# When weight conversions may run ahead in the first four steps, and a third buffer for early queries and keys

## The chip, the cores and the metric

One core of a Trainium2 chip runs the whole program. Its engines are TensorE (PE, the matrix engine; PEld is its weight load), VectorE (DVE), ScalarE (ACT), GpSimd (POOL) and SyncE (SP, which here only issues DMAs). Each works through its own queue in order; they wait for each other by semaphores. The metric is the device time of one execution in microseconds (us). Before the change it is 867.95 us, the median of three runs.

## The reference

Windowed attention, then two feed-forward networks, all in float32:

```python
def _attn_ref(q, k, v):                      # (4, 8, 576, 64)
    scores = scale * np.matmul(q, k.transpose(0, 1, 3, 2))
    mask = (rel >= 0) & (rel < 64)           # rel = query position - key position
    scores = np.where(mask, scores, -1000000000.0)
    scores = scores - np.max(scores, axis=-1, keepdims=True)
    attn = np.exp(scores)
    attn = attn / (np.sum(attn, axis=-1, keepdims=True) + 1e-09)
    return np.matmul(attn, v).astype(np.float32)

def _moe_ref(x, w1, w2, w3, w_out):          # x: 2304 x 512, d_ff 1024
    h = (x @ w1) * (x @ w2) @ w3
    return (h @ w_out).astype(np.float32)

def _moe2_ref(x, w_in, w_out):               # d_ff 2048
    h = x @ w_in
    return ((h * (1.0 / (1.0 + np.exp(-h)))) @ w_out).astype(np.float32)
```

The weights reach the kernel as float64, and it turns them into float32 itself.

## The kernel before

**Stages.** `phase_w` multiplies w3 and w_out of the first network into one matrix w' (in the code `wp`), and computes the first 14 groups of attention beside it. `phase_a`, run for six blocks of 384 tokens, multiplies by w1, w2 and w', and the remaining groups of attention run inside it. The last loop is the second network. Nothing of the order is left to a scheduler: the whole program is under a manual schedule, and every engine's queue has the order in which the Python code emits the instructions.

**A chunk** (class `Chunk`) is one 128x512 piece of a float64 weight. Its steps are: a load of 512 KB from SP (`load`, tile `words`); two ACT instructions (L114, L115, tiles `cv_b` and `cv_r`); two DVE instructions (L125 into a PSUM tile `cv_z`, L128 back into `cv_b`); and an integer addition on POOL (L132). Pieces of w3 and w_out end there, as float32 (`w3x`/`q` and `wo`). Pieces of w1 and w2 (the list `order`, 16 of them) are split further into a rounded high part (ACT, L140) and a low part, the rest (L144, tile `hl`). `words`, `cv_b`, `cv_r` have a few buffers each.

**The line** is the list of chunks in the order of their conversion. `steps_to(n, lo, keep)` advances it: step t converts chunk t with ACT, chunk t-1 with DVE and POOL, and does the high part of chunk t-3 and the low part of chunk t-4. The engine of the low part is `lo[t % len(lo)]`; `phase_w` passes (vector, gpsimd), so that an even t has it on DVE and an odd t on POOL. `line.append(None)` puts in a place without a chunk. `ready[s]` is the number of steps after which the two chunks of step s of w' are converted; `loads_to` issues loads ahead of the steps.

**w'** is accumulated in 16 steps s of two halves each (`part` 0 and 1). Ahead of each half `phase_w` calls `steps_to`, then `halves_to`, which emits attention, then two matmuls of w' (L485). In the code before, the conversions are called up to one and a half to two steps ahead of the half at hand from the start.

**Attention** goes by groups g (128 queries, two heads). A group's even half emits: scores on PE (L265, tile `s`), mask and row maximum on DVE (L279, with its read-out into `nm`), values of group g-2 on PE (L339 to L341, tile `o`, one PSUM buffer), three transposes of group g-1 on PE (L312, tile `t`), its copy on ACT (L318, `pw`), and exponentials on ACT (L290). The odd half emits the sum, reciprocal and scaling on DVE (L298, L300, L302, which writes `sm`), the copy of finished values on ACT (L342, `xr`), which frees `o`, and the loads of queries and keys of group g+2 (L223 `qp`, L227 `kp`). The first 17 groups are computed in plain float32 (`plain(g)`); their queries share a tile tag with later groups and have two buffers, their keys have two buffers `k_p`.

SP has at most eight DMAs on the way here: each issue in its queue waits for a semaphore that an issue eight places earlier raises when it lands.

Of the kernel before, what the change touches and what calls it, by code (L numbers as in the profile page):

```python
# [9 lines left out]
F32 = mybir.dt.float32  # L10
# [20 lines left out]
W12_A, W12_B = 3, 13  # L31
# [11 lines left out]
def tile_window_attention_ffn(ctx, tc, qkv, vp, mask, ident, w1, w2, w3t, w_out, w_in, w_out2, out):  # L43
# [7 lines left out]
    nc = tc.nc  # L51
# [4 lines left out]
    att = late.enter_context(tc.tile_pool(name="att", bufs=2, side="right"))  # L56
# [92 lines left out]
    line = []  # L149
    done = {"load": 0, "step": 0}  # L150

    def loads_to(n):
        while done["load"] < min(n, len(line)):
            if line[done["load"]]:
                line[done["load"]].load()
            done["load"] += 1
# [35 lines left out]

    sm = [att.tile([128, 2, 192], F32, name=f"sm{i}", tag=f"sm{i}", bufs=1) for i in range(2)]
    k_lo = [att.tile([128, 384], F32R, name=f"klo{i}", tag=f"klo{i}", bufs=1) for i in range(2)]
    k_p = [att.tile([128, 384], F32, name=f"kp{i}", tag=f"kp{i}", bufs=1) for i in range(2)]
    v_p = [att.tile([128, 320], F32, name=f"vp{i}", tag=f"vp{i}", bufs=1) for i in range(3)]
    sums_of = [att.tile([128, 2, 2], F32, name=f"es{i}", tag=f"es{i}", bufs=1) for i in range(2)]
    for t in sums_of:
# [6 lines left out]
    def plain(g):  # L205


        return g < PLAIN
# [5 lines left out]
    def load_qk(g):  # L214
        if g < NG and g not in loaded:
            loaded.add(g)
            u, c = place(g)
            if not plain(g):
                qk_raw[g] = att.tile([128, 768], F32, name=f"qk{g}", tag="qk", bufs=2)
                nc.sync.dma_start(out=qk_raw[g], in_=qkv[u, c, :, 0:768])  # L220
                return
            qk_raw[g] = att.tile([128, 768], F32, name=f"qp{g}", tag="qkhi", bufs=2)[:, 0:128]
            nc.sync.dma_start(out=qk_raw[g], in_=qkv[u, c, :, 0:128])  # L223

            for h, hs in HEADS:
                n = slice(384 + h * 192, 576 + h * 192)
                nc.sync.dma_start(out=k_p[g % 2][hs, h * 192 : h * 192 + 192], in_=qkv[u, c, hs, n])  # L227

    def load_v(g):
        if g < NG and ("v", g) not in loaded:  # L230
# [30 lines left out]
    def scores(g):  # L261
        s_ps = psa.tile([128, 2, 192], F32, name=f"s{g}", tag="s")
        t = qk_raw.pop(g) if plain(g) else qk_st.pop(g)
        if plain(g):
            nc.tensor.matmul(s_ps, lhsT=t[:, 0:128], rhs=k_p[g % 2], start=True, stop=True)  # L265
        else:
            for h in range(2):

                nc.tensor.matmul(  # L269
                    s_ps[:, h], lhsT=t[:, 128 + h * 128 : 256 + h * 128],  # L270
                    rhs=t[:, 384 + h * 192 : 576 + h * 192], start=(h == 0), stop=False,
                )
            nc.tensor.matmul(s_ps, lhsT=t[:, 0:128], rhs=k_lo[g % 2], start=False, stop=True)  # L273
        nm = att.tile([128, 2], F32, name=f"nm{g}", tag="nm", bufs=2)
        rs = att.tile([128, 2], F32, name=f"rs{g}", tag="rs", bufs=2)
        fill(2)
        for h in range(2):

            nc.vector.tensor_tensor_reduce(  # L279
                out=sm[g % 2][:, h, :], in0=s_ps[:, h, :], in1=mask_sb[:, mask_kind(place(g)[0]), 64 - 64 * h : 256 - 64 * h],  # L280
                op0=ALU.add, op1=ALU.min, scale=-(D ** -0.5), scalar=3.0e38, accum_out=nm[:, h : h + 1],
            )
        fill()
        s_st[g] = (nm, rs)
# [75 lines left out]
    def half(h):  # L360

        g, odd = divmod(h, 2)
        if not odd:
            if g < NG:
                scores(g)
            if 2 <= g <= NG + 1:
                sums.append(values(g - 2))
            if 1 <= g <= NG:  # L370
                split_t(g - 1, transposes(g - 1))
            if g < NG:
                exps(g)
            if g >= 2 and (g - 2) % (3 * NPAIR) == 3 * NPAIR - 1:
                sums.pop()()
        else:
            if g < NG:
                normalise(g)
            if sums:
                sums.pop()()  # L380
            prep_qk(g + 2)
            if g < NG:
                prep_v(g)

            for x in range(g + 2, g + 5):
                if plain(x) and x > g + 2:
                    break
                load_qk(x)
            for x in range(g + 1, g + 4):
                if g < (x - 1 if plain(x - 3) else x - 3):  # L390
                    break
                load_v(x)
# [17 lines left out]
    def phase_w():  # L410
# [22 lines left out]
        ready, i12 = [], 0  # L433
        order = (0, 1, 2, 3, 8, 9, 10, 11, 4, 5, 6, 7, 12, 13, 14, 15)
        for s in range(16):
            if s < 8:
                add(None, w_out[s * 128 : (s + 1) * 128, :], wo[:, s])
            add_w3(s)
            ready.append(len(line) + 1)
            while i12 < W12_BY[s]:  # L440
                add_w12(order[i12])
                i12 += 1
# [1 line left out]
            add_w12(order[i12])  # L444
            i12 += 1
        drain()
        ready += [W12_B + 24 + (4 if W12_B == 16 else 0)] * 2

        for t in k_p + [f32(t) for t in k_lo]:
            for h, hs in HEADS:  # L450
# [1 line left out]
        loads_to(2)  # L452
        load_qk(0)
        nc.sync.dma_start(out=mask_sb[:, 1], in_=mask[:, 1])
        loads_to(3)
        nc.sync.dma_start(out=id_sb, in_=ident)
        load_v(0)
        load_qk(1)
        loads_to(5)
        nc.sync.dma_start(out=mask_sb[:, 0], in_=mask[:, 0])  # L460
        load_v(1)
        loads_to(6)
        load_v(2)
        steps_to(ready[0])
        nc.sync.dma_start(out=mask_sb[:, 2], in_=mask[:, 2])
        half(0)
        halves[0] = 1
        acc, split_done = {}, set()
        for s in range(16):
            sw, j = divmod(s, 8)  # L470
            loads_to(ready[s + 2] + (3 if s > 1 else 0))
            if j == 0:
                for i in range(4):
                    acc[i] = accumulator(f"accw{sw}_{i}", [128, 512])
            for part in range(2):
                first = ready[s + 1 if s else 0]
                steps_to(first + (ready[s + 2] - first) * (part + 1) // 2, (nc.vector, nc.gpsimd), 3)
                halves_to(min(W_HALVES, 2 + W_HALVES * (2 * s + part + 1) // 32))
                for c in range(4):
                    if halves[0] >= min(W_HALVES, 6 * c + 10) and (0, c) not in split_done:  # L480
                        split_done.add((0, c))
                        split_x(0, c)
                fill(3)
                for i in (0, 1) if part == 0 else (2, 3):
                    nc.tensor.matmul(  # L485
                        acc[i], lhsT=w3x[s % 7][:, i * 128 : (i + 1) * 128], rhs=wo[:, j],
                        start=(j == 0), stop=(j == 7),
                    )
                    if j == 7:
                        n = sw * 4 + i  # L490
                        wp[n] = slot(f"wp{n}", f"w{16 + n}", [2, 512], F32R)
                        split(wp[n][:, 0], wp[n][:, 1], acc[i], "act", "dve")
# [58 lines left out]
    with tc.manual_schedule():  # L551
        xr = slot("xr", "xr", [4, NB])
        phase_w()
        new_pt()
        phase_a(0, lambda n: steps_to(W12_B + 24 + (n + 1) * (20 - W12_B) // 6, (nc.vector, nc.gpsimd)))
        for blk in range(1, NBLK - 1):
            phase_a(blk, lambda n: None)
        late.close()
# [206 lines left out]
```

## Time and profile before

| what | value |
|---|---|
| time, median of 3 runs (lowest to highest) | 867.95 us (867.81 to 868.38) |
| time of the execution that was profiled | 867.71 us |
| its span in the profile | 865.9 us |
| PE busy in the span | 846.7 us (98%) |
| `phase_w` (to the first matmul of L513) | 0 to 97.19 us |
| PE busy in the first 33.1 us | 20.63 us |
| PE busy from 33.1 to 97.2 us | 61.57 us |
| PE busy from 97.2 to 865.9 us | 764.49 us |
| DVE, ACT, POOL busy in the span | 436.5, 497.0, 444.7 us |

The profile shows one execution. Its span lies 1.8 us under that execution's time; the rest is around it. A timeline row has the start in us from the span's beginning, the duration in us, engine, line, operation, `out<-in`, shapes, how many instructions are merged, and in brackets the idle time of the engine just before with what ended it. Busy time of matmuls is modelled.

### The profile page before, as it was taken

The numbers are of one execution on the slowest core, as the hardware profiler recorded it, in microseconds if no ns is written. First come the engines' busy times: TensorE is split into PE (matmuls) and PEld (weight loads), VectorE is DVE, ScalarE is ACT, GpSimd is POOL, SyncE is SP. The second block draws the span as 40 slices with busy tenths as digits, with TensorE's granted clock in tenths as the row PEclk, the third lists the DMA queues.
The fourth block names the chain that finished last, engine by engine and source line by source line (L and its number), as shares of the span: only waits on it lengthen the run. The fifth ranks groups of instructions, "written<-read, shape, count | busy, mean of one in ns | idle before, by whom it ended". The sixth has DMA issues, their size and how long they took to land.

```text
span 865.9 us, 13392 instructions
## 1 busy us (share of the span) xinstructions
PE 846.7 (98%) x4362; PEld 736.0 (85%) x4362; DVE 436.5 (50%) x1160; ACT 497.0 (57%) x1243; POOL 444.7 (51%) x494
## 2 busy tenths in 40 slices
PE   5899999999999999999999999999999999999998
PEld 2445799999999999999998888888888888888896
DVE  5978877677777777675465884111111111111111
ACT  5889878788788788786766774222222222222222
POOL 4768666566666666665685886223322232223222
PEclk9999999999999999999999999999999999999999
DMA  8989333323323333320787100200020002000100
GB/s 304 323 276 276 102 103 102 120 92 110 111 92 121 110 98 116 111 92 34 249 326 272 74 1 0 98 1 1 0 98 1 1 0 74 1 1 0 49 1 25
DMA packets 43205, 85.84 MB, mean 99 GB/s; under 512 B 4864, under 2 KB 22528, under 8 KB 43136
## 3 DMA queue, kind: packets, MB, share of 16 engines
q1 hardware_dynamic: 37088, 75.55, 26.3%
q10 hardware_dynamic: 6048, 9.44, 3.0%
q8 instruction: 35, 0.57, 0.3%
q14 instruction: 34, 0.28, 0.1%
HBM read 75.53 MB, written 9.44 MB: 98 GB/s over the span
## 4 chain that ended last, share of the span: by engine, by line
PE 86%; issue 1%; DVE 1%; ACT 1%; POOL 0%; POOLq 0%; ACTq 0%; DVEq 0%
PE h L636 23%; PE o L655 23%; PE ab L513 22%; PE x L533 12%; PE t L312 2%; PE o L346 1%; PE s L269 1%; PE s L273 1%; PE o L347 1%; ACT sm L290 0%; POOL g L82 0%; DVE sm L302 0%; DVE a L521 0%; ACT p L79 0%; DVE cv_b L128 0%
## 5 line engine op out<-in xcount | busy, mean ns | idle before, releaser
L82 POOL TENSOR_TENSOR g<-sg,g 128x512 fp32r<-128x512 f32 (+1 forms) x80 | 94.7, 1184 | 249.7 <-ACT g L79 235.1
L636 PE MATMUL h<-x2t,hl 128*128 128x512 f32 (+1 forms) x960 | 213.3, 371 | 0.0
L655 PE MATMUL o<-hl,g 128*128 128x512 f32 x864 | 211.2, 391 | 0.1
L636 PEld LDWEIGHTS h<-x2t,hl 128*128 128x128 f32 x960 | 169.4, 188 | 33.9
L642 DVE TENSOR_TENSOR sg<-h,sg 128x512 f32<-128x512 f32 (+1 forms) x80 | 51.1, 638 | 288.2 <-ACT sg L641 288.2
L655 PEld LDWEIGHTS o<-hl,g 128*128 128x128 f32 x864 | 160.9, 188 | 35.6 <-POOL g L82 0.5
L641 ACT ACTIVATE sg<-h 128x512 f32<-128x512 f32 (+1 forms) x80 | 44.4, 554 | 194.8 <-PE h L636 194.7
L513 PE MATMUL ab<-xa,hl 128*128 128x384 f32 x576 | 118.9, 341 | 0.0
L513 PE MATMUL ab<-xb,hl 128*128 128x384 f32 x576 | 115.4, 334 | 0.0
L513 PEld LDWEIGHTS ab<-xb,hl 128*128 128x128 f32 x576 | 101.3, 188 | 0.0
L513 PEld LDWEIGHTS ab<-xa,hl 128*128 128x128 f32 x576 | 99.1, 188 | 0.0
L132 POOL TENSOR_TENSOR cv_b<-cv_b,cv_r 128x512 int32<-128x512 int32 x48 | 73.5, 1530 | 19.4 <-DVE cv_b L128 8.9
L79 ACT CAST g<-sg 128x512 fp32r<-128x512 f32 (+1 forms) x80 | 46.3, 578 | 63.8 <-DVE sg L642 62.9
L356 POOL TENSOR_TENSOR xr<-ot 128x128 f32<-128x128 f32 x55 | 31.5, 573 | 98.2 <-DVE ot L355 64.3
L248 POOL TENSOR_TENSOR klo<-qk,qkhi 64x192 fp32r<-64x192 f32 x110 | 67.4, 613 | 7.6 <-ACT qkhi L244 2.7
L533 PE MATMUL x<-p,wp 128*128 128x384 f32 x360 | 68.1, 339 | 0.0
L290 ACT ACTIVATE sm<-sm,nm 128x192 f32<-128x192 f32 x144 | 64.5, 449 | 3.8 <-DVE nm L279 2.5
L533 PEld LDWEIGHTS x<-p,wp 128*128 128x128 f32 x360 | 61.8, 188 | 0.1
L125 DVE TENSOR_SCALAR cv_z<-cv_b 128x512 int32<-128x512 int32 x72 | 49.5, 687 | 15.6 <-ACT cv_b L114 15.0
L114 ACT ACTIVATE cv_b<-words 128x512 f32<-128x512 f32 x72 | 48.2, 670 | 9.4 <-DMA words<-in_w_out 5.2
L128 DVE SCALAR_TENSOR_TENSOR cv_b<-words,cv_z 128x512 int32<-128x512 int32 x72 | 49.6, 688 | 3.3
L115 ACT ACTIVATE cv_r<-words 128x512 int32<-128x512 uint32 x72 | 47.7, 662 | 0.0
(81 smaller groups left out, 1235.7 us busy)
## 6 DMA issues: line engine op xcount, KB each, us to landing
qk<-in_qkv SPq DMA_DIRECT2D x55, 384.0 KB, 3.0
words<-in_w_out SPq DMA_DIRECT2D x24, 512.0 KB, 8.3
words<-in_w3t SPq DMA_DIRECT2D x16, 512.0 KB, 6.1
words<-in_w SPq DMA_DIRECT2D x16, 512.0 KB, 6.6
words<-in_w_in SPq DMA_DIRECT2D x16, 512.0 KB, 7.1
v<-in_qkv SPq DMA_DIRECT2D x55, 96.0 KB, 2.6
x2d<-x2s ACTq DMA_DIRECT2D x24, 192.0 KB, 1.9
out_x<-osb ACTq DMA_DIRECT2D x18, 256.0 KB, 2.1
```

The lines of the kernel that those rows point to most:

```text
L82: (nc.vector if eng_lo == "dve" else nc.gpsimd).tensor_tensor(out=lo, in0=src, in1=f32(hi), op=ALU.subtract)
L114: nc.scalar.activation(out=f32(self.b), in_=f32(self.high), func=AF.Copy, scale=2.0**-112)
L125: nc.vector.tensor_scalar(out=self.z, in0=b, scalar1=3, scalar2=None, op0=ALU.logical_shift_left)
L128: nc.vector.scalar_tensor_tensor(out=b, in0=self.high, scalar=-0x80000000, in1=self.z, op0=ALU.bitwise_and, op1=ALU.bitwise_or)
L132: nc.gpsimd.tensor_tensor(out=x, in0=b, in1=self.r, op=ALU.add)
L248: nc.gpsimd.tensor_tensor(out=k_lo[g % 2][hs, h * 192 : h * 192 + 192], in0=t[hs, n], in1=f32(hi[hs, n]), op=ALU.subtract)
L290: nc.scalar.activation(out=x, in_=x, func=AF.Exp, scale=-1.0, bias=nm[:, h : h + 1], accum_out=sums_of[g % 2][:, h, 0:1])
L513: nc.tensor.matmul(acc, lhsT=w[:, l, fs], rhs=x[k // 2][:, k % 2, r, :], start=(k == 0 and n == 0), stop=(k == 3 and n == 2),)
L533: nc.tensor.matmul(acc, lhsT=wp[f][:, l, o * 128 : (o + 1) * 128], rhs=p[f][:, r, :], start=(f == 0 and n == 0), stop=(f == 7 and n == 2),)
L636: nc.tensor.matmul(acc, lhsT=weights["in", f // 4, k][:, l, fs], rhs=x[:, k, r, :], start=(k == 0 and i == 0), stop=(k == 3 and i == 2),)
L642: nc.vector.tensor_tensor(out=sg, in0=acc, in1=sg, op=ALU.mult)
L655: nc.tensor.matmul(oacc[t], lhsT=g[:, l, t * 128 : (t + 1) * 128], rhs=weights["out", f][:, r, :], start=(f == 0 and i == 0), stop=(f == 1 ...
```

## The change

The conversions' lead over w' is now a function of its own: ahead of half s + part/2 the steps go to 0.5 step ahead at s = 0, growing evenly to 1.5 steps ahead at s = 4, and stay there. An empty place is put into the line after the first two chunks, so that every later chunk has a number greater by one, and the constants that count places follow (25 for 24). The keys have three buffers instead of two; the plain groups' queries get a tag of their own with three buffers; and from group three on an odd half loads up to three groups ahead instead of two, so that queries and keys of group six and later are issued one group earlier. Four early `loads_to` calls follow the new numbering.

```diff
-    k_p = [att.tile([128, 384], F32, name=f"kp{i}", tag=f"kp{i}", bufs=1) for i in range(2)]
+    k_p = [att.tile([128, 384], F32, name=f"kp{i}", tag=f"kp{i}", bufs=1) for i in range(3)]
...
-            qk_raw[g] = att.tile([128, 768], F32, name=f"qp{g}", tag="qkhi", bufs=2)[:, 0:128]
+            qk_raw[g] = att.tile([128, 128], F32, name=f"qp{g}", tag="qp", bufs=3)
...
-                nc.sync.dma_start(out=k_p[g % 2][hs, h * 192 : h * 192 + 192], in_=qkv[u, c, hs, n])
+                nc.sync.dma_start(out=k_p[g % 3][hs, h * 192 : h * 192 + 192], in_=qkv[u, c, hs, n])
...
-                if plain(x) and x > g + 2:
+                if plain(x) and x > g + (3 if g > 2 else 2):
...
             ready.append(len(line) + 1)
+            if s == 0:
+                line.append(None)
...
-        ready += [W12_B + 24 + (4 if W12_B == 16 else 0)] * 2
+        ready += [W12_B + 25] * 2
...
-        loads_to(3)
+        loads_to(4)
...
+        def lead(s):
+
+            n, rest = divmod(int(8 * s + 12 - max(0, 8 - 2 * s)), 8)
+            return ready[n] + (ready[min(n + 1, 17)] - ready[n]) * rest // 8
+
...
-                first = ready[s + 1 if s else 0]
-                steps_to(first + (ready[s + 2] - first) * (part + 1) // 2, (nc.vector, nc.gpsimd), 3)
+                steps_to(lead(s + part / 2), (nc.vector, nc.gpsimd), 3)
```

The order of PE's queue is the same in both kernels. DVE's differs in two ways. The first place is the softmax of group 0 (`s0`, `nm0`, `rs0`; `cv_z` and `cv_b` belong to conversions). Before:

```order
L279 ISA sm0_72,nm0_152<-s0_150,mask_sb_69 128x192
L279 ISA nm0_152 128x1
L125 TENSOR_SCALAR cv_z_168<-cv_b_145 128x512
L128 SCALAR_TENSOR_TENSOR cv_b_145<-words_112,cv_z_168 128x512
L125 TENSOR_SCALAR cv_z_176<-cv_b_164 128x512
L298 TENSOR_REDUCE rs0_153<-es0_81 128x2
L128 SCALAR_TENSOR_TENSOR cv_b_164<-words_120,cv_z_176 128x512
L300 RECIPROCAL rs0_153<-rs0_153 128x2
L302 TENSOR_TENSOR sm0_72<-sm0_72,rs0_153 128x384
```

The same place on DVE in the changed kernel:

```order
L279 ISA sm0_72,nm0_151<-s0_149,mask_sb_69 128x192
L279 ISA nm0_151 128x1
L298 TENSOR_REDUCE rs0_152<-es0_82 128x2
L300 RECIPROCAL rs0_152<-rs0_152 128x2
L302 TENSOR_TENSOR sm0_72<-sm0_72,rs0_152 128x384
L125 TENSOR_SCALAR cv_z_180<-cv_b_163 128x512
L128 SCALAR_TENSOR_TENSOR cv_b_163<-words_115,cv_z_180 128x512
```

The chunk's two instructions that stood between maximum and sum now stand behind the scaling, and so down to group 3. The second place is DVE from the last conversions ahead of group 8's maximum to group 9's maximum. Before:

```order
L128 SCALAR_TENSOR_TENSOR cv_b_564<-words_428,cv_z_605 128x512
L125 TENSOR_SCALAR cv_z_620<-cv_b_601 128x512
L128 SCALAR_TENSOR_TENSOR cv_b_601<-words_486,cv_z_620 128x512
L279 ISA sm0_72,nm8_618<-s8_616,mask_sb_69 128x192
...
L128 SCALAR_TENSOR_TENSOR cv_b_612<-words_527,cv_z_649 128x512
L300 RECIPROCAL rs8_619<-rs8_619 128x2
L302 TENSOR_TENSOR sm0_72<-sm0_72,rs8_619 128x384
L125 TENSOR_SCALAR cv_z_673<-cv_b_645 128x512
L128 SCALAR_TENSOR_TENSOR cv_b_645<-words_529,cv_z_673 128x512
L279 ISA sm1_73,nm9_671<-s9_669,mask_sb_69 128x192
```

The same stretch on DVE in the changed kernel:

```order
L128 SCALAR_TENSOR_TENSOR cv_b_571<-words_435,cv_z_612 128x512
L144 TENSOR_TENSOR hl_606<-cv_b_515,hl_606 128x512
L125 TENSOR_SCALAR cv_z_627<-cv_b_608 128x512
L128 SCALAR_TENSOR_TENSOR cv_b_608<-words_493,cv_z_627 128x512
L279 ISA sm0_72,nm8_625<-s8_623,mask_sb_69 128x192
...
L128 SCALAR_TENSOR_TENSOR cv_b_619<-words_534,cv_z_656 128x512
L300 RECIPROCAL rs8_626<-rs8_626 128x2
L302 TENSOR_TENSOR sm0_72<-sm0_72,rs8_626 128x384
L144 TENSOR_TENSOR hl_650<-cv_b_571,hl_650 128x512
L125 TENSOR_SCALAR cv_z_680<-cv_b_652 128x512
L128 SCALAR_TENSOR_TENSOR cv_b_652<-words_536,cv_z_680 128x512
L279 ISA sm1_73,nm9_678<-s9_676,mask_sb_69 128x192
```

Two low parts (L144) have come to DVE here, from POOL: the empty place in the line has turned the parity of every later step. Four more have come: one behind the scaling of group 9, one behind that of group 10, one behind the maximum of group 6 and one behind that of group 11. From group 12 on the sides change the other way: the two low parts that stood on DVE behind the maxima of groups 12 and 13, and the one ahead of group 11's sum, are now on POOL, as is the earliest one, behind the maximum of group 3.

## Rows read from the trace of the kernel before

**Rows 1.** Page, part 1: busy us, share of the span, instructions by engine.

```profile
PE 846.7 (98%) x4362; PEld 736.0 (85%) x4362; DVE 436.5 (50%) x1160; ACT 497.0 (57%) x1243; POOL 444.7 (51%) x494
```

**Rows 2.** Windows: stretch, its length, busy us by engine, PEclk, DMA share, GB/s.

```profile
10.00:33.00 23.00, 18.39 (x55) 8.76 (x53) 18.29 (x45) 18.34 (x45) 12.63 (x9) 1.00 1.00 347
97.20:865.90 768.70, 764.49 (x4087) 692.72 (x4084) 359.72 (x976) 421.75 (x1065) 379.27 (x432) 1.00 0.23 77
```

**Rows 3.** PE's waits to 97 us: waiter, releaser, us in all, times, longest.

```profile
PE t L312 <- DVE sm L302: 2.1, 2, 1.6
PE o L339 <- ACT xr L342: 1.9, 2, 1.6
PE t L312 <- ACT cv_r L115: 1.6, 1, 1.6
PE s L265 <- DVE rs L300: 1.5, 1, 1.5
```

**Rows 4.** PE's timeline to 34 us.

```profile
6.60 1.62 PE L265 MATMUL s<-kp,qp 128*128 128x384 f32 x2 [6.60 <-DMA kp<-in_qkv]
9.39 3.78 PE L485 MATMUL accw<-wo,q 128*128 128x512 f32 x4 [1.18 <-POOL q L132]
33.10 0.88 PE L265 MATMUL s<-kp,qp 128*128 128x384 f32 x2 [1.51 <-DVE rs L300]
```

**Rows 5.** Tile kp from 23.7 to 24.9 us: issues, issue to landing.

```profile
L227 SPq DMA_DIRECT2D kp<-in_qkv x2: 491/539/587, 23.8 to 24.3; - x2
...
DMA to landing us min/median/max: 8.6/8.8/9.0
```

**Rows 6.** Low parts: line L144 in all (ns, min/median/max), and timelines around two.

```profile
L144 DVE TENSOR_TENSOR hl<-cv_b,hl x35: 681/1033/1827, 30.1 to 532.8; 128x512 fp32r<-128x512 f32 x35
...
29.74 1.27 POOL L132 TENSOR_TENSOR w3x<-cv_b,cv_r 128x512 int32<-128x512 int32 x1 [0.29 <-ACT cv_r L115]
30.06 1.50 DVE L144 TENSOR_TENSOR hl<-cv_b,hl 128x512 fp32r<-128x512 f32 x1
...
114.57 0.42 DVE L251 TENSOR_TENSOR qkhi<-qk,qkhi 64x256 fp32r<-64x256 f32 x1 [0.24 <-ACT qkhi L244]
114.62 0.84 POOL L248 TENSOR_TENSOR klo<-qk,qkhi 64x192 fp32r<-64x192 f32 x1 [0.71 <-ACT qkhi L244]
115.03 0.98 DVE L144 TENSOR_TENSOR hl<-cv_b,hl 128x512 fp32r<-128x512 f32 x1
```

**Rows 7.** Timelines of DVE, POOL, ACT and PE from 61 to 82 us.

```profile
61.92 0.46 ACT L290 ACTIVATE sm<-sm,nm 128x192 f32<-128x192 f32 x1 [1.38 <-DVE nm L279]
63.84 0.56 DVE L302 TENSOR_TENSOR sm<-sm,rs 128x384 f32<-128x384 f32 x1
63.88 1.67 POOL L132 TENSOR_TENSOR cv_b<-cv_b,cv_r 128x512 int32<-128x512 int32 x1
64.74 0.49 PE L339 MATMUL o<-pw,vp 128*128 128x128 f32 x2 [1.59 <-ACT xr L342]
65.98 0.08 DVE L279 DVE_READ_ACCUMULATOR2_ANT nm<- 128x1 f32 x1
66.31 0.46 ACT L290 ACTIVATE sm<-sm,nm 128x192 f32<-128x192 f32 x1
...
70.37 0.08 DVE L279 DVE_READ_ACCUMULATOR2_ANT nm<- 128x1 f32 x1
71.34 0.46 ACT L290 ACTIVATE sm<-sm,nm 128x192 f32<-128x192 f32 x1
...
76.99 0.08 DVE L279 DVE_READ_ACCUMULATOR2_ANT nm<- 128x1 f32 x1
77.69 0.49 ACT L290 ACTIVATE sm<-sm,nm 128x192 f32<-128x192 f32 x1
...
81.38 0.24 ACT L342 COPY xr<-o 128x128 f32<-128x128 f32 x1
81.68 0.49 PE L339 MATMUL o<-pw,vp 128*128 128x128 f32 x2
```

More of the change, by code (lines that the diff above doesn't have):

```diff
@@ L264, in scores @@
         if plain(g):
-            nc.tensor.matmul(s_ps, lhsT=t[:, 0:128], rhs=k_p[g % 2], start=True, stop=True)
+            nc.tensor.matmul(s_ps, lhsT=t[:, 0:128], rhs=k_p[g % 3], start=True, stop=True)
         else:
@@ L458, in phase_w @@
         load_qk(1)
-        loads_to(5)
+        loads_to(6)
         nc.sync.dma_start(out=mask_sb[:, 0], in_=mask[:, 0])
         load_v(1)
-        loads_to(6)
+        loads_to(7)
         load_v(2)
@@ L554, in tile_window_attention_ffn @@
         new_pt()
-        phase_a(0, lambda n: steps_to(W12_B + 24 + (n + 1) * (20 - W12_B) // 6, (nc.vector, nc.gpsimd)))
+        phase_a(0, lambda n: steps_to(W12_B + 25 + (n + 1) * (20 - W12_B) // 6, (nc.vector, nc.gpsimd)))
         for blk in range(1, NBLK - 1):
```

## The prediction, made before the changed kernel ran

> **What bounds the kernel now.** I began with the busy times by engine: TensorE works for 846.7 of the 865.9 us of the span, and no other engine comes over 497 [rows 1]. The table of windows then says where its 19 idle microseconds lie. From 97.2 us to the end it is busy for 764.49 of 768.70 us [rows 2]. The change touches little behind that point, so what it can win or lose is the time at which `phase_w` ends, and that is set by PE's waits ahead of it. The list of PE's waits gives them one by one [rows 3], and its timeline the places [rows 4]: 6.60 us for the first keys, 1.18 for the first pieces of w', 1.6 for each of the transposes `t` of groups 0 and 1, 1.51 ahead of the scores `s` of group 4 at 33.10, and 1.59 ahead of the values `o` of group 7 at 64.74 [rows 4, 7]. The reader should hold two of these apart from the rest. The wait at 33.10 is put down to DVE, but group 4's keys were issued at 23.8 and 24.3 us and needed 8.6 to 9.0 us to land [rows 5], the later one at 24.3 + 8.6 = 32.9: it is a DMA that ends last there. And in the stretch from 10 to 33 us the DMA engines are busy all the time, at 347 GB/s [rows 2]; SP's issues wait for landings there, not for an engine.
>
> **The change, part one: the lead in the first four steps.** It moves two instructions of each conversion from between a group's maximum and its sum to behind the scaling, in groups 0 to 3. The two waits of `t` in this stretch, 1.6 + 1.6 = 3.2 us [rows 3], are waits for that softmax (the first is named after ACT, which had conversions in front of the exponentials). I take both as gone. Not all of it need reach the scores of group 4, since a lead of half a step puts the pieces of w' nearer to their matmuls, and PE has waited for such pieces once, for 1.18 us [rows 4]. Between none of the 3.2 and all, I take 1.45, about half. But the order of SP's queue is unchanged up to group 4's keys, and a queue that waits for landings at full DMA load is not moved by an earlier softmax. The keys land at 33 as before, so PE's wait there grows from 1.51 to 1.51 + 1.45 = 3.0 us, and this part brings **0**. If it did not, nothing else would be late before 64 us, where all of PE's idle time together is under 1 us (97.19 - 33.10 us less the busy time of that stretch and the wait of `o`).
>
> **Part two: third buffers and issuing queries and keys one group earlier from group 6 on.** PE has no wait for a key or query between 33.10 and 97.2 us [rows 3]: the list has none for a DMA behind the first. What is not waited for can't be brought forward to any use: **0**. The loads leave SP earlier and compete with the pieces of weights; I allow 0.3 us either way.
>
> **Part three: the parity.** The empty place makes every later step's number greater by one, and so changes the engine of the low part L144. Six low parts come to DVE between 44 and 83 us, and seven leave it, the most of them after 83 us. On POOL nobody waited for them; on DVE they stand in front of the maxima and behind the scalings of groups 8 to 11, the chain on which PE's values depend: maximum, exponentials on ACT, then (ACT's queue being in order) the copy `xr` that frees the only buffer of `o`. In this stretch ACT has little to spare, and the rows say how much:
>
> Group 8: the low part stands ahead of the maximum. It costs at least its shortest duration, 0.68 us [rows 6]. ACT stood idle for 1.38 us waiting for just that maximum at 61.92 [rows 7], so all of it passes on: exponentials 0.68 late, and `o` at 64.74, which waited 1.59 for ACT, with them.
>
> Groups 9, 10 and 11: a low part directly behind the scaling L302 of the group before. At the first of these places an addition of POOL starts at 63.88, while DVE's scaling runs from 63.84 to 64.40, and takes 1.67 us instead of the 1.27 of the undisturbed one [rows 6, 7]: it waited and went when the scaling was done. DVE's next instruction was one that read PSUM. Now it is a low part with two operands in SBUF. What happens between two such instructions the trace shows twice: at 30.06 a low part on DVE took 1.50 us beside an addition of POOL that ended at 31.01, so that 0.55 us of it lie behind that end, and at 115.03 a low part which stood back to back with another two-operand instruction let POOL's waiting one (114.62 to 115.46) go first, and ended at 116.01, again 0.55 behind [rows 6]. So POOL goes first, and the price is 1.27 + 0.55 = **1.82 us**; the longest low part on DVE in the trace took 1.827 [rows 6].
>
> From these the slack is taken. Group 9: its maximum is out at 65.98 + 0.08 = 66.06, its exponentials start at 66.31, slack 0.25: 0.68 + 1.82 - 0.25 = 2.25 late. Group 10: 70.45 against 71.34, slack 0.89: 2.25 + 1.82 - 0.89 = 3.18. Group 11: 77.07 against 77.69, slack 0.62: 3.18 + 1.82 - 0.62 = **4.38** [rows 7]. At the end of this stretch `xr` ends at 81.62 and `o` starts at 81.68 [rows 7], with no slack, so PE is 4.38 us late there, and behind it PE is full. The low parts that leave DVE after 83 us don't give it back, since PE doesn't wait for DVE there.
>
> The bounds of this price: 0.68 a piece if DVE keeps its turn, which gives 0.68, then 0.68 + 0.68 - 0.25 = 1.11, 1.11 + 0.68 - 0.89 = 0.90, 0.90 + 0.68 - 0.62 = 0.96 us; and 1.83 for all four, 1.83, 3.41, 4.35, 5.55 us. I take the middle case since the row at 115.03 is the nearest: the same pair of engines, back to back, with POOL waiting.
>
> The Trainium skill has a rule on this, in "SBUF — State Buffer", section "SBUF: two separate sides": the port pair that VectorE and GpSimd share is an exclusive lock, whichever starts first has it for its whole instruction, and the other is blocked. The rows at 30.06 and 115.03 agree with it. It does not say who goes first when both wait; with the lock to POOL the sum is the 4.38 above, with the lock to DVE 0.96. It speaks against this change.
>
> **The sum.** 0 + 0 + 4.38 us on the profiled execution: 867.71 + 4.38 = 872.1. That execution lies 0.24 under the median of 867.95, so against the median 867.95 + 4.38 = **872.3 us**, 0.5% slower. A measurement of this kernel can tell about 0.2%, here 1.7 us.
>
> **Rivals.** (B) *DVE keeps its turn.* Each low part costs its own 0.68 and no more: +0.96, 868.9 us, not slower in a way that can be measured. For it speaks that most low parts are near the 1.03 median, not at the maximum [rows 6]; against it the row at 115.03. It decides if POOL's addition is not yet waiting when the scaling ends, that is if POOL is over 0.5 us later than before.
>
> (C) *The clock.* PE's first instructions took twice as long as later ones: scores 1.62 us at 6.60 against 0.88 at 33.10, as at the lower of the two levels (the four matmuls of w' at 9.39 took 3.78, 0.95 each) [rows 4], though the column of the granted clock reads 1.00 [rows 2]. Both followed idle time. If the wait of 3.0 us at group 4's scores brings that back, it costs about 1.62 - 0.88 = 0.74 for the scores and half of 3.78, 1.89, for four matmuls: 2.6 us on top, 874.9. Against it speaks that the wait of 1.51 at 33.10 did nothing of the kind (0.88 behind it) [rows 4]. By the Trainium skill, "TensorE: Matmul & The Clock Gate", section "Part 1: The HAM clock gate", idleness of PE lowers its clock; no row here shows a wait of 3 us behind the first.
>
> (D) *The keys come when PE does.* If SP issues group 4's keys earlier, since something else than landings held it, the wait of 3.0 us goes: -2.96. With B that is 868.9 - 2.96 = 866.0, the one way to a faster kernel that I see; with the forecast's low parts 872.3 - 2.96 = 869.4, no difference. It decides if the keys are issued before about 22 us. Against it: the DMA share of 1.00 and 347 GB/s [rows 2]. For it: I followed SP's waits from the order, and they could be loosened where a tile is freed earlier.
>
> **How the numbers follow.** Forecast 0.55; B 0.20; C 0.08; D 0.17, of which 0.14 on the faster side and 0.03 within 0.2% of before. Faster: 0.14. Within 0.2%: B and the rest of D, 0.23. Slower: the forecast and C, 0.63. The range goes from D with B, 866.0 us, to the forecast with all four low parts at 1.83, 867.95 + 5.55 = 873.5; C and part of D lie outside, some 0.16 to 0.2.
>
> **What would show it.** The first step is right if the two waits of `t` below 23 us are gone, the wait ahead of group 4's scores has grown to about 3 us, and group 4's keys still land near 33. The third is right if DVE shows six low parts between 44 and 83 us, three of them near 1.8 us right behind L302 with an addition of POOL ending 0.55 us ahead of their ends, and if PE's waits of `o` for `xr` have grown from 1.9 us [rows 3] to about 6, so that the first matmul of L513 stands near 101.5 us instead of 97.19. Low parts of 0.7 to 1.0 us there make B right. Scores of group 4 in 1.6 us make C right. A first L513 ahead of 96 us would make the whole sum wrong, by its first step, and a wait of PE for something that this text doesn't name would too.

## The result, and the profile after

The changed kernel takes 875.37 us (median of six, 872.79 to 876.89) against 867.34 for the kernel before, measured beside it (six runs, 866.31 to 868.38): a ratio of 1.0083, 95% interval 1.0071 to 1.0096. It is slower, as forecast, but by more: 872.3 us was predicted, and 875.37 lies outside the range of 866.0 to 873.5. The profiled execution took 875.55 us with a span of 873.8, 7.9 more than before.

PE's waits in the changed kernel (waiter, releaser, us in all, times, longest) answer to [rows 3]:

```profile
PE s L265 <- DMA kp<-in_qkv: 10.6, 3, 6.8
PE o L339 <- ACT xr L342: 4.2, 5, 1.6
PE t L312 <- DVE sm L302: 1.4, 1, 1.4
PE accw L492 <- POOL q L132: 1.1, 1, 1.1
```

The two waits of `t` below 23 us are gone; the one of 1.4 us that is left stands at 89.47 us, at the transposes of group 11. The kernel before waited there too, for 0.55 us; it is the second of the two waits for L302 in [rows 3]:

```profile
83.11 0.52 PE L312 MATMUL t<-id_sb,sm 128*128 128x128 f32 x3 [0.55 <-DVE sm L302]
```

The waits of `o` have become five, 4.2 us in all, where the forecast had about 6. The first line holds the first keys (6.78), 0.55 ahead of group 2's scores and 3.23 us ahead of group 4's scores, where [rows 4] had 1.51. PE's timeline around that place (start, duration, engine, line, operation, `out<-in`, shapes, merged instructions, idle time before):

```profile
25.53 3.60 PE L492 MATMUL accw<-wo,q 128*128 128x512 f32 x8
32.36 1.62 PE L265 MATMUL s<-kp,qp 128*128 128x384 f32 x2 [3.23 <-DMA kp<-in_qkv]
33.77 0.64 PE L339 MATMUL o<-pw,vp 128*128 128x128 f32 x2
34.20 0.64 PE L340 MATMUL o<-pw,vp 128*128 128x128 f32 x2
34.62 0.53 PE L341 MATMUL o<-pw,vp 128*128 128x64 f32 x2
34.94 0.85 PE L312 MATMUL t<-id_sb,sm 128*128 128x128 f32 x3
35.58 3.18 PE L492 MATMUL accw<-wo,q 128*128 128x512 f32 x4
38.60 3.60 PE L492 MATMUL accw<-wo,w3x 128*128 128x512 f32 x8
```

The scores take 1.62 us, as the very first ones did [rows 4], and four matmul instructions of w' 3.18, where eight take 3.60 three microseconds later. The granted clock says the same. In the windows (stretch, its length, busy us and instructions of PE, PEld, DVE, ACT and POOL, granted clock, DMA share, GB/s), it is 0.50 from 32 to 36 us, the lower of the two levels, and there is a second such place between 87 and 95:

```profile
29.00:32.00 3.00, 0.13 (x1) 0.00 (x0) 2.56 (x5) 2.45 (x6) 2.70 (x3) 0.89 0.98 335
32.00:36.00 4.00, 3.64 (x12) 2.99 (x13) 1.90 (x6) 0.17 (x1) 1.88 (x2) 0.50 0.75 241
36.00:39.00 3.00, 3.00 (x5) 1.08 (x4) 1.23 (x3) 3.00 (x9) 1.27 (x1) 0.63 0.91 253
...
90.00:95.00 5.00, 5.00 (x11) 2.24 (x10) 4.69 (x12) 4.36 (x11) 4.52 (x4) 0.72 0.63 203
104.88:873.80 768.92, 764.57 (x4087) 692.83 (x4084) 358.66 (x975) 422.14 (x1065) 380.74 (x433) 1.00 0.23 76
```

The last line answers to the second of [rows 2]: from the first matmul of the first network on (now L520, at 104.88 instead of 97.19) the kernel needs 768.92 us, before 768.70. Nearly the whole loss, 7.69 of 7.9 us, lies in `phase_w`. The second fall comes behind two waits close together:

```profile
84.95 0.81 PE L265 MATMUL s<-kp,qp 128*128 128x384 f32 x2
87.17 0.49 PE L339 MATMUL o<-pw,vp 128*128 128x128 f32 x2 [1.41 <-ACT xr L342]
...
89.47 0.87 PE L312 MATMUL t<-id_sb,sm 128*128 128x128 f32 x3 [1.42 <-DVE sm L302]
90.14 4.93 PE L492 MATMUL accw<-wo,w3x 128*128 128x512 f32 x8
```

The low parts are where the forecast put them. DVE and POOL behind group 8's scaling, to be set beside 63.84 and 63.88 in [rows 7]:

```profile
66.27 0.56 DVE L302 TENSOR_TENSOR sm<-sm,rs 128x384 f32<-128x384 f32 x1
66.30 1.66 POOL L132 TENSOR_TENSOR cv_b<-cv_b,cv_r 128x512 int32<-128x512 int32 x1 [0.80 <-DVE rs L300]
66.74 1.77 DVE L144 TENSOR_TENSOR hl<-cv_b,hl 128x512 fp32r<-128x512 f32 x1
```

POOL's addition starts beside the scaling and ends at 67.96, DVE's low part ends at 68.51, 0.55 behind it. Behind groups 9 and 10 the low part took 1.76 us each time:

```profile
72.52 1.76 DVE L144 TENSOR_TENSOR hl<-cv_b,hl 128x512 fp32r<-128x512 f32 x1
78.29 1.76 DVE L144 TENSOR_TENSOR hl<-cv_b,hl 128x512 fp32r<-128x512 f32 x1
```

PE's timelines of before and after, laid side by side, give the ledger. Group 3's scores start 2.46 us earlier than before, group 4's only 0.74 earlier (the keys). From there to group 5's scores 9.68 us pass instead of 6.82: the first fall of the clock, 2.86. The delay is then +2.12, and still +2.11 at the transposes `t` of group 6; at those of group 11 it is +6.36, so 4.25 come in the stretch of the low parts. From there to the transposes of group 12 it grows by 1.34, the second fall. -0.74 + 2.86 + 4.25 + 1.34 = 7.71, and L520 stands 7.69 later. (Where the low parts are on DVE and no fall comes, the stretch from group 11 to group 12 takes 0.30 less than before; against that, the second fall is worth 1.64.)

### The profile page after: what moved, and what is told of

Read it like the earlier page. It is cut to its first block, busy times and chain, and to the rows that moved or that the text cites. A ratio compares the mean times of both kernels' runs of the same rounds, so it can differ in the third digit from the quotient of the medians.

```text
span 873.8 us, 13386 instructions
## 1 busy us (share of the span) xinstructions
PE 852.0 (98%) x4362; PEld 738.3 (85%) x4362; DVE 439.2 (50%) x1161; ACT 497.5 (57%) x1243; POOL 444.3 (51%) x495
## 4 chain that ended last, share of the span: by engine, by line
PE 87%; POOL 3%; DMA 3%; ACT 2%; DVE 2%; issue 2%; SPq 0%; POOLq 0%; DVEq 0%
PE h L643 23%; PE o L662 22%; PE ab L520 20%; PE x L540 11%; PE accw L492 2%; PE t L312 2%; DMA kp<-in_qkv 1%; PE o L346 1%; PE s L269 1%; PE s L273 1%; POOL klo L248 1%; PE s L265 1%; PE o L347 1%; ACT sm L290 1%; DVE cv_b L128 1%
## 5 line engine op out<-in xcount | busy, mean ns | idle before, releaser
L520 PE MATMUL ab<-xa,hl 128*128 128x384 f32 x576 | 118.8, 340 | 0.0
L520 PE MATMUL ab<-xb,hl 128*128 128x384 f32 x576 | 115.4, 334 | 0.0
L520 PEld LDWEIGHTS ab<-xb,hl 128*128 128x128 f32 x576 | 101.3, 188 | 0.0
L520 PEld LDWEIGHTS ab<-xa,hl 128*128 128x128 f32 x576 | 99.0, 188 | 0.0
L125 DVE TENSOR_SCALAR cv_z<-cv_b 128x512 int32<-128x512 int32 x72 | 49.4, 687 | 16.0 <-ACT cv_b L114 15.2
L128 DVE SCALAR_TENSOR_TENSOR cv_b<-words,cv_z 128x512 int32<-128x512 int32 x72 | 49.5, 688 | 3.4
L279 DVE CUSTOM_DVE_ANT_0 sm<-s,mask_sb 128x192 f32<-128x192 f32 x144 | 45.3, 352 | 6.1 <-PE s L265 4.2
```

Source lines behind the costliest of these rows:

```text
L125: nc.vector.tensor_scalar(out=self.z, in0=b, scalar1=3, scalar2=None, op0=ALU.logical_shift_left)
L128: nc.vector.scalar_tensor_tensor(out=b, in0=self.high, scalar=-0x80000000, in1=self.z, op0=ALU.bitwise_and, op1=ALU.bitwise_or)
L520: nc.tensor.matmul(acc, lhsT=w[:, l, fs], rhs=x[k // 2][:, k % 2, r, :], start=(k == 0 and n == 0), stop=(k == 3 and n == 2),)
```

## The experiments

Theory 1 in the expectations is the ledger: low parts, and two falls of the clock that follow waits. Its first rival puts all that comes late behind 60 us down to the first fall and takes the low parts to be harmless. The table gives each profiled execution against the profiled execution of before, in us: where group 4's scores start and how long PE waited for them; what the stretch to group 5's scores takes over 6.82 (first fall); the growth of the delay between the transposes of groups 6 and 11 (low parts); what the stretch between those of groups 11 and 12 takes over 5.35 (second fall); and the first matmul of the first network. The next column has the ratio of times with its interval. A dash stands where the stretch was longer for another wait, not for the clock.

| kernel | scores 4 | wait | first fall | low parts | second fall | L513/L520 | ratio to before |
|---|---|---|---|---|---|---|---|
| before | 0 | 1.51 | 0 | 0 | 0 | 0 | 1 |
| changed | -0.74 | 3.23 | 2.86 | 4.25 | 1.34 | +7.69 | 1.0083 (1.0071 to 1.0096) |
| changed, again | -0.52 | 3.17 | 1.66 | 4.25 | 2.65 | +8.01 | 1.0066 (1.0049 to 1.0083) |
| changed, sides swapped back | +0.06 | 3.06 | 1.66 | 0.02 | 0 | +1.71 | 1.0013 (1.0000 to 1.0025) |
| before, sides swapped | +0.75 | 2.01 | 0 | 4.24 | 1.02 | +5.99 | 1.0047 (1.0033 to 1.0061) |
| changed, three low parts moved | +1.09 | 4.05 | 3.00 | 1.73 | -0.30 | +5.48 | 1.0034 (1.0021 to 1.0047) |
| changed, two buffers | +0.16 | 3.38 | 1.67 | 4.24 | 1.19 | +7.24 | 1.0061 (1.0048 to 1.0073) |
| before, third buffers | +1.00 | 1.93 | 1.66 | 0.01 | 0 | +2.65 | 0.9998 (0.9990 to 1.0007) |
| changed, wait filled | -0.28 | 0.44 | 0 | 4.25 | -0.30 | +3.88 | 1.0059 (1.0040 to 1.0078) |
| changed, keys earlier | -3.29 | 0 | - | 4.24 | 2.70 | +6.37 | 1.0049 (1.0037 to 1.0061) |
| both: keys, sides | -4.14 | 0 | - | 0 | 0 | -1.17 | 1.0004 (0.9995 to 1.0014) |
| changed, all low parts moved | +0.12 | 2.98 | 0 | 2.01 | -0.30 | +3.19 | 1.0047 (1.0035 to 1.0059) |
| changed, two waits filled | +1.00 | 1.53 | 0 | 4.15 | -0.27 | +5.11 | 1.0047 (1.0035 to 1.0060) |
| before, wait filled | -0.39 | 0 | 0 | 0.02 | 0 | -0.38 | 0.9998 (0.9989 to 1.0008) |

The landing of the first keys alone moved the start of a profile by up to 0.84 us (6.60 to 7.44), so the first column is no finer than that.

**The sides of the low parts.** First the changed kernel with the two engines of `lo` swapped, so that each low part is back where it was:

```diff
-                steps_to(lead(s + part / 2), (nc.vector, nc.gpsimd), 3)
+                steps_to(lead(s + part / 2), (nc.gpsimd, nc.vector), 3)
...
-        phase_a(0, lambda n: steps_to(W12_B + 25 + (n + 1) * (20 - W12_B) // 6, (nc.vector, nc.gpsimd)))
+        phase_a(0, lambda n: steps_to(W12_B + 25 + (n + 1) * (20 - W12_B) // 6, (nc.gpsimd, nc.vector)))
...
-            steps_to(begin + H5[n], (nc.vector, nc.gpsimd))
+            steps_to(begin + H5[n], (nc.gpsimd, nc.vector))
```

> The changed kernel with the two engines of the low parts swapped, so that every low part is back on the engine that it had before. Theory 1 (the low parts on DVE cost 4.2 us between 57 and 90 us and bring on the second fall of the clock, 1.3 us; the first fall of the clock at group 4's scores costs 2.9, against 0.7 won ahead of it): -0.7 + 2.9 = +2.1 us over the kernel before, about 869.5 us, scores of group 4 still in 1.6 us, no fall of the clock near 90 us. Rival (the low parts are harmless and all that comes late behind 60 us follows from the first fall): unchanged, about 875.

Measured: 869.6 us (12 runs, 867.2 to 870.78). The time is as expected, and the 4.25 us and the second fall are gone. The first fall is there, but smaller than expected: 1.66 instead of 2.9, with the scores at 0.88 us, not 1.6, since the clock fell only behind them. Then the same swap in the kernel before, and nothing else:

> The kernel before with the engines of the low parts swapped, nothing else. Theory 1: no wait of 3 us and no fall of the clock at group 4's scores; three low parts behind L302 at 1.76 us; +4.2 us, and +1.3 more if the clock falls near 85 us: 871.5 to 872.9. Rival (low parts harmless): within 1 us of before, under 868.4.

Measured: 872.6 us (870.51 to 873.84) against 868.04. The 4.24 us and the second fall come without any change of lead or buffers; low parts on DVE behind L302 in its trace:

```profile
65.38 1.77 DVE L144 TENSOR_TENSOR hl<-cv_b,hl 128x512 fp32r<-128x512 f32 x1
71.16 1.77 DVE L144 TENSOR_TENSOR hl<-cv_b,hl 128x512 fp32r<-128x512 f32 x1
76.93 1.76 DVE L144 TENSOR_TENSOR hl<-cv_b,hl 128x512 fp32r<-128x512 f32 x1
```

Both runs speak for the ledger: swapping sides takes the term away from one kernel and gives it to the other, to 0.02 us. The rival is out. The lead has no run to itself; the sides swapped back leave it with the third buffers, and that costs 1.71 us in the profile, the size of the first fall.

**Work or collision.** In the changed kernel the three low parts behind the scalings of groups 8, 9 and 10 were moved behind the next conversion's two DVE instructions; same engine, same work, another neighbour:

```diff
+                if t in (26, 28, 30):
+                    fill(2)
                 line[t - 4].low_part(lo[t % len(lo)])
```

> The changed kernel with three low parts alone moved behind the next conversion's two instructions on DVE: those directly behind the scalings of groups 8, 9 and 10. All other places of all queues are as in the changed kernel. Theory 1 (collision with POOL's waiting addition): 0.68 instead of 1.76 us each, and the delay between the transposes of groups 6 and 11 falls from 4.24 to about 1.0 us, the sum of 0.68 a piece less the slack; 3.2 us less than the changed kernel beside it, more where the second fall of the clock goes too. Rival (more work on DVE in this stretch costs, wherever it stands): above 3 us of delay there.

Measured: 870.53 us (870.27 to 873.07) against 873.58 for the changed kernel beside it, 3.05 less. DVE's low parts from 60 us on, and what POOL did beside the last two:

```profile
64.03 0.68 DVE L144 TENSOR_TENSOR hl<-cv_b,hl 128x512 fp32r<-128x512 f32 x1
70.10 0.68 DVE L144 TENSOR_TENSOR hl<-cv_b,hl 128x512 fp32r<-128x512 f32 x1
74.86 0.68 DVE L144 TENSOR_TENSOR hl<-cv_b,hl 128x512 fp32r<-128x512 f32 x1
...
79.44 1.01 POOL L82 TENSOR_TENSOR xb<-xr,xb 128x384 fp32r<-128x384 f32 x1
79.58 1.42 DVE L144 TENSOR_TENSOR hl<-cv_b,hl 128x512 fp32r<-128x512 f32 x1
...
82.55 1.27 POOL L132 TENSOR_TENSOR w3x<-cv_b,cv_r 128x512 int32<-128x512 int32 x1 [0.41 <-DVE cv_b L128]
...
82.85 1.52 DVE L144 TENSOR_TENSOR hl<-cv_b,hl 128x512 fp32r<-128x512 f32 x1
```

Two of the three (70.10, 74.86) fell to 0.68; the third, at 79.58, met another instruction of POOL, which ran from 79.44 to 80.45, and ended 0.55 us behind it, as in the changed kernel. So did the one at 82.85, behind POOL's 83.82. The delay between the transposes of groups 6 and 11 went from 4.25 to 1.73, not to the 1.0 expected: 0.84 of what is left comes at group 11's transposes, where the low part at 82.85, which was not moved, took 1.52. So 2.5 of the 4.25 us are the place of three instructions, and the amount of work on DVE is the smaller part. An earlier form of this edit, which moved every low part of the first stage and also other conversions with them, was less clean:

> The changed kernel with each low part on DVE in the first stage put behind the conversion's two instructions in the queue instead of ahead of them, so that it no longer stands directly behind the scaling L302. The same low parts stay on DVE. Theory 1 (three of them cost 1.76 us since a waiting addition of POOL goes first): they take about 0.7 us, -1.1 us each, -3.2 in all, and -1.3 if the clock then doesn't fall near 90 us: 870.9 to 872.2. Rival (what costs is that DVE has more work, wherever it stands): the same 875.

It gave 872.65 us (870.63 to 873.14): more than the 870.9 to 872.2 expected. The waits at the values of groups 8 and 9 vanished, but between group 5's scores and group 7's the delay grew by 1.38 us, and from group 6's values to group 7's by 1.78, most of it in a wait of 1.06 at group 9's scores. That the conversions which had moved along did this was not tried by itself.

**The first fall of the clock.** Four matmuls of identity and mask (eight instructions in the trace, since each of these float32 matmuls shows as two) were put into PE's wait, written to a tile that the scores overwrite:

```diff
+        if g == 4:
+            for _ in range(4):
+                nc.tensor.matmul(s_ps, lhsT=id_sb, rhs=mask_sb[:, 0:2, 0:192], start=True, stop=True)
```

> The changed kernel with four matmuls of identity and mask put ahead of group 4's scores, into the tile that the scores overwrite: some 3.2 us of work in the time in which PE waits for the keys. It adds work and changes nothing of the result. Theory 1 (PE's idle time there lowers the clock): scores of group 4 in 0.8 us at about 32.4, granted clock 1.00 from 32 to 39 us, -2.9 us against the changed kernel, about 872.5. Rival (the scores and what follows are slow because of the late keys or of what DMA does): scores in 1.6 us as in the changed kernel, 875 or more.

Measured: 872.92 us (870.99 to 876.84). The scores come at 32.82, half a microsecond later than in the changed kernel, and take 0.88 us:

```profile
29.64 2.74 PE L266 MATMUL s<-mask_sb,id_sb 128*128 128x384 f32 x8
32.82 0.88 PE L268 MATMUL s<-kp,qp 128*128 128x384 f32 x2 [0.44 <-DMA kp<-in_qkv]
...
34.15 0.50 PE L315 MATMUL t<-id_sb,sm 128*128 128x128 f32 x3
34.49 1.88 PE L495 MATMUL accw<-wo,q 128*128 128x512 f32 x4
```

Work that adds 2.74 us to PE makes the rest of `phase_w` 3.8 us earlier than in the changed kernel (+3.88 against +7.69): the first fall, 2.86, and the second, 1.64, neither of which this execution had, less 0.46 by which the scores came later and 0.23 lost by group 7's. The mean granted clock of each whole execution was measured too: three of these six have 1.000 (870.99 to 872.25 us), where no execution of the changed kernel comes over 0.998; the other three (0.998, 0.996 and 0.993) fell somewhere all the same. The keys were as late as ever. In time it is 2.5 us less than the first measurement of the changed kernel, though not clearly less than the second (below). With a second piece of such work ahead of group 11's transposes:

> The changed kernel with matmuls of identity and mask in two of PE's waits: four ahead of group 4's scores as before, and two (1.2 us) between group 10's values and group 11's transposes, into the tile that the transposes overwrite. Theory 1: the granted clock stays at 1.00 in all of 29 to 100 us, the low parts still cost 4.2, and the whole is about 4 us over the kernel before, 871.5 to 872.5, with a narrower spread than the changed kernel. Rival (the falls have another cause than PE's idleness): 874 to 876, with falls at both places.

Measured: 871.69 us (871.36 to 872.91), a spread of 1.6 us where the changed kernel beside it had 4.6 (871.71 to 876.34). Their intervals against before overlap, though (1.0035 to 1.0060 and 1.0049 to 1.0083), so that the gain is not clear. At the two filled places the clock stayed up. The profiled execution had a fall at a third place, which the expectation did not allow for: behind group 7's wait, which is in the kernel before as well [rows 7]:

```profile
66.32 0.49 PE L345 MATMUL o<-pw,vp 128*128 128x128 f32 x2 [1.58 <-ACT xr L348]
...
67.15 0.85 PE L318 MATMUL t<-id_sb,sm 128*128 128x128 f32 x3
67.79 4.86 PE L498 MATMUL accw<-wo,q 128*128 128x512 f32 x8
```

**Not the same in every execution.** The changed kernel was run again:

> The changed kernel once more, beside the others of this call. Theory 1: 4.2 us between group 6's and group 11's transposes for the low parts, as in every run that has them; the falls of the clock near 33 and near 90 us come in most executions but not in all, so that the total lies between +3.5 us (none) and +8 us (both) over before, 871.5 to 876. Rival (falls come in every execution alike): 875 to 876.

Measured: 873.58 us (871.71 to 876.34), ratio 1.0066 (1.0049 to 1.0083). Its profiled execution was its slowest, with both falls, +8.01. The mean granted clock goes from 0.998 in the two fastest (871.71 and 871.82) to 0.993 in the slowest, and in the first measurement, with its larger ratio of 1.0083, from 0.996 to 0.994. So the falls differ in size and number from one execution to the next, but by this measure none of these twelve was free of them: 0.998 is what the profile with sides swapped back has, with its one fall of 1.66. Without a fall the ledger gives 868.01 - 0.74 + 4.25 = 871.5; the three executions at 1.000 of the kernel with one wait filled lie around that. The fastest, 871.71, comes near it with a mean clock below 1.000: single executions differ by a microsecond or two without any fall (the kernel before at 1.000: 866.74 to 868.66), so that one time alone does not tell of falls.

**The third buffers**, alone on the kernel before (the diff's lines for `k_p`, `qp` and the loads' condition), and taken out of the changed kernel:

> The kernel before with the third buffers for keys and queries alone, and the loads of group six and later one group earlier. Theory 1 (nothing waits for those loads): within 0.2% of before. Rival (the earlier loads take DMA time from pieces of weights): slower by more than 2 us.

> The changed kernel without the third buffers: keys and queries have two again and their loads stand where they stood; lead and empty place as in the changed kernel. Theory 1: as the changed kernel, 873 to 877 us, with the two falls of the clock where they were. Rival (the loads of group six and later, issued early, are what costs): under 871.

Measured: 868.13 us beside 868.14 for before, and 873.75 us. They do nothing that shows. But the first of these profiles has a fall of the clock in what is otherwise the kernel before, behind a wait of 1.93 us, with a granted clock of 0.84 from 32 to 36 us and 0.73 from 36 to 40:

```profile
34.10 0.98 PE L265 MATMUL s<-kp,qp 128*128 128x384 f32 x2 [1.93 <-DVE rs L300]
34.88 0.63 PE L339 MATMUL o<-pw,vp 128*128 128x128 f32 x2
```

Whether that sets the spread of the kernel before (866.59 to 871.69 in 17 executions) was tried with two matmuls in its wait:

> The kernel before with two such matmuls (1.6 us) ahead of group 4's scores, in its wait of 1.5 to 2.0 us there. Theory 1 (the kernel before has this fall too, in some executions, as the run with third buffers alone had it): its slower executions go, median 867.0 to 867.5, about 0.1% under before. Rival (the spread of before is something else): the same median and the same spread as before.

Measured: 867.96 us (867.21 to 869.24) beside 868.01 (866.74 to 870.69). The median did not move, ratio 0.9998 (0.9989 to 1.0008); the spread is narrower, but this shows nothing clear. That the clock goes with the slower executions of the kernel before does show: of the 17 beside this run, the four at 870.0 us or more have a mean granted clock of 0.998 or 0.997, all others 0.999 or 1.000. Where in the kernel it fell is not known.

**The keys.** Group 4's queries and keys (and group 5's) were issued one group earlier, group 4's ahead of two pieces of weights more:

```diff
-                if plain(x) and x > g + (3 if g > 2 else 2):
+                if plain(x) and x > g + (3 if g > 0 else 2):
```

> The changed kernel, but an odd half loads three groups ahead from group one on instead of from group three on: in SP's queue group 4's queries and keys stand behind those of group 3, ahead of two pieces of w' more than before, and group 5's one group earlier too. Nothing else in any queue moves. Theory 1 (the wait of 3.2 us at group 4's scores is for these keys alone, and lowers the clock): that wait and the slow stretch behind it go, 3.2 + 2.9 = 6.1 us less than the changed kernel, if no piece of w' comes late in its place; about 869, and not above 871. Rival (DMA is full, so that the pieces of w' behind them come late by as much): PE waits for w' instead, the clock falls all the same, 874 to 876.

Measured: 872.09 us (871.37 to 874.28): 3 above the expected 869, over its bound of 871 and under the rival's 874. The wait for the keys is gone, the scores start at 29.81, and PE waits right behind them, for ACT, and ACT for a piece of w3:

```profile
29.81 0.81 PE L265 MATMUL s<-kp,qp 128*128 128x384 f32 x2
32.68 0.49 PE L339 MATMUL o<-pw,vp 128*128 128x128 f32 x2 [2.06 <-ACT xr L342]
```

```profile
29.61 0.67 ACT L114 ACTIVATE cv_b<-words 128x512 f32<-128x512 f32 x1 [1.30 <-DMA words<-in_w3t]
```

The rival was right as to the wait, though this one brought no fall. The second fall was there, with 2.70. With the sides swapped back as well:

> The changed kernel with both: group 4's and 5's queries and keys one group earlier, and the engines of the low parts swapped back. Theory 1: no wait at group 4's scores, no fall of the clock, no low part behind L302 on DVE: the 2.5 us that the lead wins by group 3 reach the end, up to 3.5 if PE's former wait of 1.5 goes too; 864.0 to 865.5 us, below the kernel before. Rival (a later wait, for a piece of w' or at group 7's values, takes the place): 867 to 868.

Measured: 868.45 us (12 runs, 866.51 to 871.25) beside 868.14. Of the 4.14 us by which group 4's scores came earlier, waits of `o` for ACT at groups 2, 3 and 4 (1.03, 0.66 and 0.84) took back 2.53, and by 50 us 1.17 is left; the median shows none of it. It is no faster than the kernel before, and no run here was, beyond the noise. The rival's 867 to 868 was nearer than the 864.0 to 865.5 expected.

## Why the prediction was right and wrong

**The direction and most of the mechanism were right.** That the parity costs some 4 us, and that third buffers are worth nothing, is borne out by a run with that part alone. That POOL's waiting addition goes first behind L302, with 1.82 us as the price (measured 1.77, 1.76, 1.76), is borne out by the run that moved three low parts. That the lead wins nothing, since PE waits for the keys, is what the profile shows: PE came to group 4's scores 2.46 us earlier, not 1.45, and waited 3.23, not 3.0, for keys that were there at 32.36, not 33. With the falls of the clock left out, the ledger gives 867.95 - 0.74 + 4.25 = 871.5, against 872.3 predicted.

**The sum of the low parts, 4.38, was met (4.25), but partly by luck.** Counted from the transposes of group 6, the values of groups 7, 8, 9 and 10 came 0.33, 1.00, 1.74 and 3.38 us late, where the forecast has 0.68, 2.25, 3.18 and 4.38. Group 8's low part was priced at no less than its 0.68; on DVE it put off the maximum by only 0.34 (2.53 us from the start of the L128 ahead of it, before 2.19). And the slack taken off was ACT's alone, though PE had not waited at the values of groups 8 and 9 before. The 0.87 that is missing to 4.25 came at group 11's transposes, where the wait for DVE grew from 0.55 to 1.42. The prediction said that PE doesn't wait for DVE behind 83 us, and so passed over the second wait in its own [rows 3], at 83.11. A low part behind group 11's maximum, not priced, took 1.52 us there; that it alone made the wait grow was not tried. So two errors of opposite sign nearly cancelled. Two smaller misreadings change no number of the sum: the L125 behind the scaling writes PSUM and does not read it, and five low parts leave DVE, not seven (L144 on DVE: 35 before, 36 after).

**The step that failed is rival C, the clock.** The sum put the clock at nothing. The wait of group 4's scores was forecast to grow from 1.51 to 3.0 us, and it was seen that such a wait might bring the lower clock, at 2.6 us. It did: the first fall cost 2.86 us in the first profile and 1.66 in the second, and a second fall 1.34 and 2.65. The chance of 0.08 rested on "the wait of 1.51 did nothing of the kind": one wait half as long, in one execution, was taken as evidence on a wait twice as long, when the only row on longer idleness, the first scores at 6.60 [rows 4], took 1.62 us as at the lower level (the column of the granted clock reads 1.00 over those first 10 us too, so that it does not tell of them). With C's 874.9 the predicted time would have been within the spread that was measured, 872.79 to 876.89; the range ended ahead of it. The rule cited from the Trainium skill ("TensorE: Matmul & The Clock Gate", "Part 1: The HAM clock gate") pointed the right way, and the trace agrees: a granted clock of 0.50 from 32 to 36 us behind the idle time.

**A second fall was not thought of.** With the low parts on DVE two neighbouring waits are longer, 1.41 us at group 10's values and 1.42 at group 11's transposes, and five of the six profiles that have both waits show a fall there, of 1.02 to 2.70 us (the kernel with the wait at 32 us filled has them too, 1.38 and 1.42, and no fall). With the sides swapped back, neither run that has the low parts on POOL there shows one. The delays were added up as if PE's speed were given.

**Rival D's size was wrong.** Keys that come earlier were priced at the whole wait, 2.96 us. The runs with earlier keys show that DMA is full (a share of 1.03 from 29 to 40 us in the one with sides swapped back): the time goes to the weights behind them, and 1.17 us is left in the best execution.

**What stays open.** Which waits bring the lower clock is not settled. Waits of 3.0 to 4.1 us at group 4's scores had it in five of six profiles (not in the one where all low parts were moved, 2.98 us); waits of 1.5 to 2.0 us at the same place in one of four (with third buffers alone, 1.93), and one of 2.06 right behind, in the run with earlier keys, did not. That PE's idle time is what matters rests on the two profiles in which work filled the wait at group 4's scores and the clock stayed up there. The same program can run with and without a fall: the mean granted clock of the kernel before lies between 1.000 and 0.996, that of the kernel before with sides swapped between 1.000 and 0.995.

## What to carry to other kernels

Two two-operand instructions in a row on DVE are not one price plus another where POOL waits with an operation of its own (1.76 us here for one of 0.68): look at what POOL has queued at that moment, and count its whole duration. A number that counts places and also picks an engine by its parity makes an empty place a change of engines; compare the order of every engine, not only the lines that were meant to change. A row of waits that counts two has two places: look up both before saying that an engine isn't waited for. And where a change lets PE arrive earlier at a transfer that it can't hurry, the wait that grows there can cost the speed of what follows: price it from the rows at the lower clock, and let the range reach there.

## What the runs showed of the hardware that was not expected

A stretch at the lower clock can follow waits of under 2 us (1.93 at group 4's scores; 1.58 at group 7's values; 1.41 and 1.42 near 88 us), though the same waits left it at 1.00 in other executions and kernels. One such stretch cost 1.0 to 3.0 us. Work put into such a wait, with no use of its own, kept the clock at 1.00 there in both profiles of the changed kernel that have it. The kernel with two pieces of it took 871.69 us against 873.58 for the same kernel without, though the intervals of the two overlap.
